# Seven block products for the first projection, and a partial sum that ScalarE copies into PSUM

## The chip, the core and the metric

The kernel runs on one core of a Trainium2 chip. The time is the device time of one execution in microseconds (us); of several runs the median is told. A profile is one execution taken by the hardware profiler. Its engines are PE (TensorE's matrix products), PEld (TensorE's weight loads, which overlap PE), DVE (VectorE), ACT (ScalarE), POOL (GpSimd) and SP, whose queue issues most of the transfers.

## What is computed

Three stages follow each other on 6016 rows of 256 channels; this is the reference without its setup:

```
qn = q / (np.linalg.norm(q, axis=1, keepdims=True) + 1e-06)     # q, k, v: (1, 6016, 256)
kn = k / (np.linalg.norm(k, axis=1, keepdims=True) + 1e-06)
s = kn.transpose(0, 2, 1) @ qn / tau                            # 256 x 256
a = softmax(s)                                                  # over the last axis
x = v @ a                                                       # 6016 x 256
h = x @ w_in                                                    # w_in 256 x 2048
g = np.where(h >= 1, h, np.where(h <= -1, 0, (h + 1) ** 2 / 4))
x = g @ w_out                                                   # w_out 2048 x 256
xn = x / sqrt(mean(x * x, -1) + 1e-6) * rms_g
gate = xn @ w_gate; val = xn @ w_val                            # 256 x 1536 each
out = (gate * sigmoid(gate) * val) @ w_out2                     # w_out2 1536 x 256
```

The weights arrive as doubles and are brought to single precision on the chip. The change concerns `h = x @ w_in` and, to a smaller part, `gate` and `val`.

## The kernel before

**Start.** The scores are summed while q and k arrive; the softmaxed 256 x 256 matrix is multiplied into `w_in`, so that v goes straight through one combined weight, held in SBUF as a rounded part `w1h` and its remainder `w1l`.

**Three products for one.** Every factor is kept as a rounded part and its remainder, and a product of 128 x 128 weights with n columns is three matmuls: high by high, remainder by high, high by remainder. n is the number of rows of one tile: 12 tiles stand in 6 pairs, of which pairs 0 to 4 have n = 512 and pair 5 has n = 448.

**The first network (`network_1`).** For a pair, `prep_v` transposes v on DVE and splits it. `block_A` (line 708) makes one 128 x n block of h from two such products (two blocks of channels, six matmuls), 16 blocks for each tile. Then ACT forms relu(h/2 + 1/2) and squares it, DVE takes max(h, 1) and the smaller of the two (line 722), ACT copies the rounded part `gh`, DVE subtracts for `gl`. `block_B` (line 742) multiplies the block by `w_out` into the sums `y`, two products of three matmuls.

**The second network (`network_2`).** After the norm, `combine` forms from the four blocks of a pair (two channel blocks by two tiles) the seven sums that a seven-product scheme for 2 x 2 blocks needs. For every two blocks of `w_gate` and `w_val` the stored weight has seven blocks too (`to_seven` makes them once and keeps them in DRAM, `load_seven` fetches them). `seven_units` then makes a chain of seven products, p1, p2, p6, p7, p5, p3, p4, in three PSUM buffers: X1 (gx, vx) takes p1, p6, p5 and p3 on top of each other, Z (gz, vz) takes p2, S (gy, vy) takes p7 and p4. In between ACT copies X1 to SBUF (`copied`, line 863) and DVE adds Z or S to a copy (`add`, line 868). A chain gives four blocks: p1 + p2, and three others. `block_D` (line 948) multiplies the gated result by `w_out2`.

**Order.** `ORDER` runs the networks of the pairs in turn: 1 of pairs 0 and 1, 2 of pair 0, 1 of pair 2, 2 of pair 1 and so on. Within a chain the string `CHAIN` sets the wanted order on PE: c is the chain's next product, t one of the two products left over from the chain before (p3, p4), d a product of `block_D`. Every instruction gets a due time; a list planner written into the kernel then places all instructions of PE, ACT, DVE, POOL and SP with its own costs and with buffers from numbered slots (four PSUM slots `mm` for h, X1, Z and S, twenty SBUF slots `tmp`, and others). Each engine executes its instructions in the order so fixed.

Of the kernel before, what the change touches and what calls it, by code (L numbers as in the profile page):

```python
# [15 lines left out]
P = 128  # L16
# [46 lines left out]
def tile_channel_attention_two_ffn(  # L63
# [422 lines left out]
    n_op = {cls: SLOTS[cls] for cls in ("stage", "op", "rows")}  # L486
    first_op = {"stage": 0, "op": n_op["stage"], "rows": n_op["op"] + n_op["stage"]}
# [66 lines left out]
    for t in range(2):  # L554
        V[t] = [Buf("op", f"v{p}{t}", slot=2 * t + i) for i, p in enumerate("hl")]
# [22 lines left out]
    def narrow(key, src, at, step, on_act, into=None):  # L578
        x = Buf("stage", f"wide_{key}", [P, NC, TOK])
# [32 lines left out]
    for p in range(NF2 // 2):  # L612
        kept_dram["wd", p] = drp.tile([P, 4 * C], F32, name=f"kept_wd{p}")
        for nm in "gv":
            kept_dram[nm, p] = drp.tile([P, 2, 7, P], F32, name=f"kept_{nm}{p}")

    def to_rows(kind, j, src, at, step, on_act, eng):
        x = narrow(f"{kind}{j}", src, at, step, on_act)
        w = Buf("rows", f"{kind}{j}", [P, 2, 2, C], F32R)
# [14 lines left out]
    def to_seven(kind, p, src, at, step):  # L634
        f = Buf("stage", f"f{kind}{p}", [P, 8, P])
        h = Buf("stage", f"h{kind}{p}", [P, 7, P], F32R)
        narrow(f"{kind}{p}", src, at, step, True, f)
        for i, (o, a, b, how) in enumerate((
# [9 lines left out]
            at, [(f, s) for s in range(1, 8)], [h], [h])  # L648
# [83 lines left out]
    def block_B(t, f, c, w, at):  # L732
        _, n = tiles[t]
        gh, gl = G[t, f]
        if (f, c) == (0, 0):
            Y[t] = Buf("yo", f"y{t}")
        y = Y[t]

        def mm():
            cs = slice(c * P, (c + 1) * P)  # L740
            for i, (h, x) in enumerate(((0, gh.t), (1, gh.t), (0, gl.t))):
                nc.tensor.matmul(  # L742
                    y.t[:, c, :n], w.t[:, f % 2, h, cs], x[:, :n],
                    start=(f == 0 and i == 0), stop=(f == NF1 - 1 and i == 2),
                )
        op("PE", pe(3, n), mm, at, [gh, gl, (w, 0), (w, 1)], [(y, c)], [y] if (f, c) == (0, 0) else [])
        if (f, c) == (NF1 - 1, NC - 1):
# [7 lines left out]
    def norm(t, at, step):  # L755
# [5 lines left out]
        ps = Buf("mm", f"ms{t}")  # L761
        m = Buf(None, f"m{t}")
# [42 lines left out]
    def combine(q, at, step):  # L805
        _, n = tiles[2 * q]
        x0, x1 = X[2 * q], X[2 * q + 1]
        got = XO[q] = {}
        when = [at]

        def keep(name, b, c=None):
            w = got[name] = Buf("op", f"x{name}_{q}", [P, 2, TOK], F32R)
# [8 lines left out]
        def mix(name, a, b):  # L821
            d = Buf("tmp", f"d{name}_{q}")
# [186 lines left out]
    conversions.sort()  # L1009
# [4 lines left out]
    for due, _, kind, which, src in [c for c in conversions if c[2] in ("wi", "wo")] + late:  # L1014
# [238 lines left out]
```

## Time and profile before

| | |
|---|---|
| median of three runs | 1135.0 us (1134.12 to 1135.71) |
| the profiled execution | 1134.83 us, span of its instructions 1133.1 us |
| PE busy | 1109.2 us, 98% of the span, 4950 instructions |
| PEld, DVE, ACT, POOL busy | 930.7, 820.0, 749.6, 86.4 us |
| granted TensorE clock, mean | 0.994 |

A row of busy time adds up the recorded lengths of instructions. On PE, and to a smaller degree on ACT and DVE, an instruction begins before the recorded end of the one ahead of it, so rates are better read from starts. The matmuls of the scores and of the norms of q and k are recorded as two each, so the profile counts 97 more than the 4853 matmuls of the program.

### The profile page before, as it was taken

The page shows a single profiled execution, that of the slowest core. Times are in us where ns is not written, and L with a number is a line of the kernel's source. Part 1 is how long each engine was busy: PE and PEld are TensorE (multiplying, and loading weights), DVE is VectorE, ACT ScalarE, POOL GpSimd, SP SyncE. Part 2 cuts the span into 40 slices and gives each one's busy share as a digit, 9 for nine tenths or more (in the row PEclk, how much of TensorE's full clock was granted, in tenths as well). Part 3 has the DMA queues.
Part 4 walks back from the last instruction along what each step waited for, and adds up shares of the span by engine and source line. Part 5 has one row for each costly group of instructions (what it writes and reads, how often), then busy time and mean ns, then how long its engine had stood idle before and what let it go on. Part 6 is the DMA issues. An engine that isn't in the chain of part 4 may idle for free.

```text
span 1133.1 us, 13952 instructions
## 1 busy us (share of the span) xinstructions
PE 1109.2 (98%) x4950; PEld 930.7 (82%) x4950; DVE 820.0 (72%) x1311; ACT 749.6 (66%) x1325; POOL 86.4 (8%) x84
## 2 busy tenths in 40 slices
PE   7799999999999999999999999999999999999996
PEld 6678888888888888888888888888888998888995
DVE  5989989969985448886446977445968545976664
ACT  6589898987666666666666556666557566555552
POOL 0000244313100002000000100000200000200000
PEclk9999999999999999999999999999999999999998
DMA  9766575577536413425432432532442412444742
GB/s 346 238 174 180 189 258 217 196 201 260 163 115 185 80 56 135 155 97 123 124 75 102 167 135 53 183 63 89 149 167 103 126 56 92 161 153 155 216 149 33
DMA packets 138854, 167.65 MB, mean 148 GB/s; under 512 B 103712, under 2 KB 103712, under 8 KB 138784
## 3 DMA queue, kind: packets, MB, share of 16 engines
q1 hardware_dynamic: 135072, 166.29, 47.2%
q10 hardware_dynamic: 3712, 0.46, 0.3%
q8 instruction: 39, 0.64, 0.2%
q14 instruction: 31, 0.25, 0.1%
HBM read 142.21 MB, written 24.51 MB: 147 GB/s over the span
## 4 chain that ended last, share of the span: by engine, by line
PE 93%; DMA 4%; DVE 1%; SPq 1%; ACT 0%; issue 0%; DVEq 0%; ACTq 0%
PE y L742 23%; PE h L708 22%; PE o L948 17%; PE vx L855 9%; PE gx L855 9%; PE gy L855 4%; PE vy L855 4%; PE vz L855 2%; PE gz L855 2%; DMA qk<-in_k_dram 1%; DMA wide<-in_moe_w_in_dram 1%; DMA qk<-in_q_dram 1%; PE w_ps L682 1%; SPq L180 1%; DMA soon<-in_moe_w_out_dram 1%; PE w_ps L405 0%
## 5 line engine op out<-in xcount | busy, mean ns | idle before, releaser
L722 DVE SCALAR_TENSOR_TENSOR g<-h,g 128x512 f32<-128x512 f32 (+1 forms) x192 | 129.1, 676 | 144.9 <-ACT g L720 144.9
L742 PE MATMUL y<-gh,wo 128*128 128x512 f32 (+1 forms) x768 | 233.5, 385 | 0.0
L717 ACT ACTIVATE g<-h 128x512 f32<-128x512 f32 (+1 forms) x192 | 112.8, 587 | 121.5 <-PE h L708 121.3
L948 PE MATMUL o<-uh,wd 128*128 128x512 f32 (+1 forms) x576 | 175.6, 386 | 0.0
L742 PEld LDWEIGHTS y<-gh,wo 128*128 128x128 f32 x768 | 144.2, 188 | 27.3 <-DVE wo L143 0.2
L708 PE MATMUL h<-vh,w1h 128*128 128x512 f32 (+1 forms) x384 | 148.1, 386 | 0.3 <-ACT w1h L414 0.3
L708 PE MATMUL h<-vl,w1h 128*128 128x512 f32 (+1 forms) x384 | 148.0, 385 | 0.3 <-DVE vl L143 0.3
L742 PE MATMUL y<-gl,wo 128*128 128x512 f32 (+1 forms) x384 | 148.0, 385 | 0.1
L143 DVE TENSOR_TENSOR gl<-g,gh 128x512 fp32r<-128x512 f32 (+1 forms) x192 | 129.2, 678 | 7.4 <-ACT gh L725 7.1
L948 PEld LDWEIGHTS o<-uh,wd 128*128 128x128 f32 x576 | 108.1, 188 | 20.4
L720 ACT ACTIVATE g<-g 128x512 f32<-128x512 f32 (+1 forms) x192 | 119.0, 621 | 4.2
L725 ACT ACTIVATE gh<-g 128x512 fp32r<-128x512 f32 (+1 forms) x192 | 117.0, 611 | 6.8 <-DVE g L722 6.8
L708 PE MATMUL h<-vh,w1l 128*128 128x512 f32 (+1 forms) x384 | 116.8, 385 | 0.0
L948 PE MATMUL o<-ul,wd 128*128 128x512 f32 (+1 forms) x288 | 111.2, 386 | 1.5 <-DVE ul L143 1.5
L708 PEld LDWEIGHTS h<-vh,w1h 128*128 128x128 f32 x384 | 72.1, 188 | 14.6 <-ACT w1h L414 0.7
L708 PEld LDWEIGHTS h<-vl,w1h 128*128 128x128 f32 x384 | 72.1, 188 | 14.2 <-DVE vl L143 0.6
L742 PEld LDWEIGHTS y<-gl,wo 128*128 128x128 f32 x384 | 72.1, 188 | 13.7 <-DVE gl L143 0.4
L708 PEld LDWEIGHTS h<-vh,w1l 128*128 128x128 f32 x384 | 72.1, 188 | 13.6 <-DVE w1l L415 0.3
L948 PEld LDWEIGHTS o<-ul,wd 128*128 128x128 f32 x288 | 54.1, 188 | 12.1 <-DVE ul L143 1.9
L855 PE MATMUL gy<-xt,gw 128*128 128x512 f32 (+1 forms) x216 | 60.0, 386 | 0.0
L855 PE MATMUL vx<-xt,vw 128*128 128x512 f32 (+1 forms) x216 | 60.0, 386 | 0.0
L855 PE MATMUL gx<-xb,gw 128*128 128x512 f32 (+1 forms) x216 | 60.0, 386 | 0.0
(181 smaller groups left out, 1840.1 us busy)
## 6 DMA issues: line engine op xcount, KB each, us to landing
gw<-kept_g SPq DMA_DIRECT2D x36, 896.0 KB, 4.7
vw<-kept_v SPq DMA_DIRECT2D x36, 896.0 KB, 4.7
wo<-kept_wo SPq DMA_DIRECT2D x40, 512.0 KB, 4.0
wd<-kept_wd SPq DMA_DIRECT2D x36, 512.0 KB, 3.6
vin<-in_v_dram SPq DMA_DIRECT2D x80, 64.0 KB, 3.9
out_dram<-ob SPq DMA_DIRECT2D x80, 64.0 KB, 2.0
qk<-in_q_dram SPq DMA_DIRECT2D x9, 512.0 KB, 10.2
qk<-in_k_dram SPq DMA_DIRECT2D x9, 512.0 KB, 10.2
```

Source lines behind the costliest of these rows:

```text
L143: return eng.tensor_tensor(out=dst_lo, in0=src, in1=hi.bitcast(F32), op=ALU.subtract)
L180: nc.sync.dma_start(out=xv[32 * a:32 * a + 32, c, :n // 32, :], in_=src[a, c])
L682: nc.tensor.matmul(got[b].t, x[:, c * P:(c + 1) * P], w[:, c, :], start=(i == 0), stop=(i == len(terms) - 1),)
L708: nc.tensor.matmul(ps.t[:, :n], w[:, c, f * P:(f + 1) * P], x[:, c, :n], start=(i == 0), stop=(i == len(terms) - 1),)
L717: op("ACT", act(n), lambda: nc.scalar.activation(out=r.t[:, :n], in_=ps.t[:, :n], func=AF.Relu, bias=0.5, scale=0.5), at, [ps], [r], [r])
L720: op("ACT", act(n), lambda: nc.scalar.activation(out=r.t[:, :n], in_=r.t[:, :n], func=AF.Square), at, [], [r])
L722: op("DVE", dve(n), lambda: nc.vector.scalar_tensor_tensor(out=r.t[:, :n], in0=ps.t[:, :n], scalar=1.0, in1=r.t[:, :n], op0=ALU.max, op1=A ...
L725: op("ACT", act(n), lambda: nc.scalar.activation(out=gh.t[:, :n], in_=r.t[:, :n], func=AF.Copy), at, [r], [gh], [gh])
L742: nc.tensor.matmul(y.t[:, c, :n], w.t[:, f % 2, h, cs], x[:, :n], start=(f == 0 and i == 0), stop=(f == NF1 - 1 and i == 2),)
L855: nc.tensor.matmul(ps.t[:, :n], w.t[:, h, a, :], b.t[:, e, :n], start=(start and i == 0), stop=(i == 2), skip_group_check=True,)
L948: nc.tensor.matmul(o.t[:, c, :n], w.t[:, f % 2, h, cs], x[:, :n], start=(nth == 1 and i == 0), stop=(nth == NF2 and i == 2),)
```

## The change

From pair 2 on the first projection uses the scheme of seven products as well. `turn_pair` transposes v of both tiles and `combine` forms the seven sums; `to_seven` makes the seven blocks of each of the eight pairs of weight blocks from `w1h + w1l` (one DVE addition, four on POOL, one copy on ACT, one subtraction on DVE) during the second network of pair 0, writes them to DRAM, and `network_1s` fetches them for each pair and runs eight chains `h` (buffers hx, hz, hy) of seven products. Pairs 0 and 1 keep `network_1`.

In all chains but one (g, pair 4, first) p1 is now copied by ACT into Z's own PSUM buffer, and p2 accumulates onto it, where before p1 was copied to SBUF and DVE added p2. The planner gives such a Z only slots of PSUM that matmuls have already written in at least as many columns (`written`, `seed`). `CHAIN` changes from `ccttccddcdd` to `cttccdcdcdd`, `CHAIN_1` is new, and the slots of the classes `stage` and `op` are merged.

```
-CHAIN = "ccttccddcdd"
-SLOTS = {"mm": 4, "yo": 2, "stage": 7, "op": 19, "rows": 4, "tmp": 20, "seven": 3}
-RESERVE = {"tmp": 4, "mm": 1}
+CHAIN = "cttccdcdcdd"
+CHAIN_1 = "cdttccddcddcddd"
+PLAIN = 2
+H_AT = (70.0, 16.0)
+PREP_S = 50.0
+SLOTS = {"mm": 4, "yo": 2, "op": 24, "rows": 4, "tmp": 20, "seven": 4}
+RESERVE = {"tmp": 4, "mm": 1, "op": 4}
...
-    def to_seven(kind, p, src, at, step):
+    def to_seven(kind, p, at, step, src=None):
...
+            op("DVE", dve(TOK), lambda: nc.vector.tensor_tensor(
+                out=f.t[:, :4, :].rearrange("p (k s) c -> p k (s c)", k=NC),
+                in0=w1h[:, :, cols].bitcast(F32), in1=w1l[:, :, cols].bitcast(F32), op=ALU.add),
...
         def p1(at):
             product(X1, A11, "b11", True, at)
-            copied("a", at)
+            if not seeded:
+                copied("a", at)
+                return
+            Z.seed = n
+            op("ACT", act(n), lambda: nc.scalar.activation(
+                out=Z.t[:, :n], in_=X1.t[:, :n], func=AF.Copy), at, [X1], [Z], urgent=30)

         def p2(at):
-            product(Z, A12, "b21", True, at)
-            take(1, 0, add("a", Z, at), at)
+            product(Z, A12, "b21", not seeded, at)
+            take(1, 0, Z if seeded else add("a", Z, at), at)
...
+    def turn_pair(q, at, step):
...
+            for c in range(NC):
+                op("DVE", dve(n), lambda c=c, x=x, r=r: nc.vector.transpose(
+                    out=r.t[:, c, :n], in_=x.t[:, c, :n]), at, [x], [(r, c)])
+                at += step
+            raw.append(r)
+        combine("v", q, *raw, at, step)
+
+    def network_1s(q):
+        turn_pair(q, phase_at[1, q] - PREP_S, STEP)
...
+                squared(t, f, d, at)
+                for c in range(NC):
+                    pend.append((us, lambda at, c=c: block_B(t, f, c, rows[p], at)))
...
+        for p in range(NF1 // 2):
+            load_seven("h", p, now - LEAD["seven"])
+            rows[p] = load_rows("wo", p, now + LEAD["wd"])
+            chain = seven_units("h", q, p, take(p))
+            fill.extend(pend)
+            pend.clear()
+            for what in CHAIN_1:
...
-        (network_1, network_2)[net - 1](q)
+        if net == 2:
+            network_2(q)
+        elif q < PLAIN:
+            network_1(q)
+            if q == 0:
+                for p in range(NF1 // 2):
+                    to_seven("h", p, phase_at[1, PLAIN] - H_AT[0] + H_AT[1] * p, STEP)
+        else:
+            network_1s(q)
...
-            f = sorted(free[b.cls].values())
+            f = sorted(t for i, t in free[b.cls].items() if b.cls != "mm" or written[i] >= b.seed)
```

Counted in the two built programs, PE has 96 matmuls fewer, ACT 116 instructions more, DVE 37 more, POOL 32 more and SP 48 transfers more. Three places show how the order moves.

PE before, second network of pair 2, from p1 of the gate's fourth chain on (gx_3 and gz_3 are X1 and Z of that chain, vx_2 and vy_2 belong to the chain ahead):

```order
L855 MATMUL gx_3_5917<-xb_2_4613,gw_5810 128x512 x3
L855 MATMUL gz_3_5925<-xb_2_4626,gw_5810 128x512 x3
L855 MATMUL vx_2_5835<-xb_2_4763,vw_5755 128x512 x3
L855 MATMUL vy_2_5869<-xt_2_4753,vw_5755 128x512 x3
L855 MATMUL gx_3_5917<-xt_2_4697,gw_5810 128x512 x3
L855 MATMUL gy_3_5950<-xt_2_4727,gw_5810 128x512 x3
L948 MATMUL o_5649<-uh_2_10_5889,wd_5514 128x512 x2
L948 MATMUL o_5649<-ul_2_10_5921,wd_5514 128x512
L948 MATMUL o_5649<-uh_2_10_5889,wd_5514 128x512 x2
L948 MATMUL o_5649<-ul_2_10_5921,wd_5514 128x512
L855 MATMUL vx_3_5970<-xb_2_4613,vw_5876 128x512 x3
L855 MATMUL gx_3_5917<-xt_2_4704,gw_5810 128x512 x3
```

and the same place after:

```order
L877 MATMUL gx_3_6063<-xb_2_4760,gw_5891 128x512 x3
L975 MATMUL o_5863<-uh_1_11_5987,wd_5613 128x512 x2
L975 MATMUL o_5863<-ul_1_11_6007,wd_5613 128x512
L975 MATMUL o_5863<-uh_1_11_5987,wd_5613 128x512 x2
L975 MATMUL o_5863<-ul_1_11_6007,wd_5613 128x512
L877 MATMUL vx_2_5990<-xb_2_4899,vw_5808 128x512 x3
L975 MATMUL o_5848<-uh_1_00_6024,wd_5613 128x512 x2
L975 MATMUL o_5848<-ul_1_00_6039,wd_5613 128x512
L877 MATMUL vy_2_6048<-xt_2_4891,vw_5808 128x512 x3
L877 MATMUL gz_3_6080<-xb_2_4770,gw_5891 128x512 x3
L877 MATMUL gx_3_6063<-xt_2_4839,gw_5891 128x512 x3
L877 MATMUL gy_3_6116<-xt_2_4870,gw_5891 128x512 x3
```

Before, p1 (to gx_3) and p2 (to gz_3) stood side by side and nine matmuls stood between p1 and p6; now fifteen matmuls stand between p1 and p2, and p6 follows p2.

PE before, first network of pair 3 (h are blocks of the first projection, y the sums of the second):

```order
L708 MATMUL h_3_4951<-vh_4358,w1h 128x512
L708 MATMUL h_3_4951<-vl_4382,w1h 128x512
L708 MATMUL h_3_4951<-vh_4358,w1h 128x512
L708 MATMUL h_3_4951<-vl_4382,w1h 128x512
L708 MATMUL h_3_4951<-vh_4358,w1l 128x512 x2
L742 MATMUL y_4908<-gh_1_4912,wo_4497 128x512 x2
L742 MATMUL y_4908<-gl_1_4931,wo_4497 128x512
L742 MATMUL y_4908<-gh_1_4912,wo_4497 128x512 x2
L742 MATMUL y_4908<-gl_1_4931,wo_4497 128x512
```

and the first network of pair 3 after (hx_4, hz_4 and hy are X1, Z and S of a chain, vb and vt the sums of v):

```order
L877 MATMUL hx_4_5247<-vb_3_4336,hw_5068 128x512 x3
L762 MATMUL y_5062<-gh_4_5225,wo_4931 128x512 x2
L762 MATMUL y_5062<-gl_4_5238,wo_4931 128x512
L762 MATMUL y_5062<-gh_4_5225,wo_4931 128x512 x2
L762 MATMUL y_5062<-gl_4_5238,wo_4931 128x512
L877 MATMUL hx_3_5149<-vb_3_4475,hw_4905 128x512 x3
L762 MATMUL y_5062<-gh_5_5236,wo_4931 128x512 x2
L762 MATMUL y_5062<-gl_5_5251,wo_4931 128x512
L877 MATMUL hy_3_5215<-vt_3_4572,hw_4905 128x512 x3
L877 MATMUL hz_4_5266<-vb_3_4343,hw_5068 128x512 x3
```

Six matmuls to a block of h have given way to single products of a chain, with the products to y in between; fifteen matmuls stand between p1 (to hx_4) and p2 (to hz_4).

ACT before, first network of pair 3 (relu from h, then the square in place, then the rounded part gh):

```order
L725 ACTIVATE gh_8_5200<-g_8_5167 128x512
L717 ACTIVATE g_9_5209<-h_9_5192 128x512
L720 ACTIVATE g_9_5209<-g_9_5209 128x512
L725 ACTIVATE gh_8_5230<-g_8_5188 128x512
L717 ACTIVATE g_9_5239<-h_9_5213 128x512
L720 ACTIVATE g_9_5239<-g_9_5239 128x512
L725 ACTIVATE gh_9_5253<-g_9_5209 128x512
L717 ACTIVATE g_10_5262<-h_10_5243 128x512
L720 ACTIVATE g_10_5262<-g_10_5262 128x512
L725 ACTIVATE gh_9_5274<-g_9_5239 128x512
```

and after, from the second copy of chain 4 to the first copy of chain 5:

```order
L885 ACTIVATE hc_4_5299<-hx_4_5247 128x512
L738 ACTIVATE g_6_5304<-hc_3_5211 128x512
L738 ACTIVATE g_9_5311<-hz_4_5266 128x512
L745 ACTIVATE gh_6_5316<-g_6_5273 128x512
L740 ACTIVATE g_6_5304<-g_6_5304 128x512
L745 ACTIVATE gh_7_5327<-g_7_5287 128x512
L740 ACTIVATE g_9_5311<-g_9_5311 128x512
L885 ACTIVATE hu_4_5336<-hx_4_5247 128x512
L745 ACTIVATE gh_6_5348<-g_6_5304 128x512
L901 ACTIVATE hz_5_5366<-hx_5_5338 128x512
L738 ACTIVATE g_8_5373<-hu_4_5336 128x512
L745 ACTIVATE gh_9_5378<-g_9_5311 128x512
```

A chain has three copies of X1 (to hz, hc and hu) between the three instructions for each of its four blocks; between two copies stand one to six of these.

## Rows read from the trace of the kernel before

**Rows 1.** The page: engines, busy time, share of the span, instructions.

```profile
PE 1109.2 (98%) x4950; PEld 930.7 (82%) x4950; DVE 820.0 (72%) x1311; ACT 749.6 (66%) x1325; POOL 86.4 (8%) x84
```

**Rows 2.** Who waited for whom, PE: us in total, times, longest.

```profile
PE a_ps L457 <- ACT s_sb L451: 6.9, 2, 5.3
PE s_ps L304 <- DMA qk<-in_k_dram: 5.8, 2, 4.3
PE o L948 <- DVE ul L143: 1.5, 1, 1.5
PE h L708 <- ACT w1h L414: 0.3, 1, 0.3
PE h L708 <- DVE vl L143: 0.3, 1, 0.3
PE n_ps L361 <- DVE acc L334: 0.3, 1, 0.3
```

**Rows 3.** Chain that ended last: start us, us; 512, then 448 columns.

```profile
336.03 2.72 PE h L708 x12
341.47 2.72 PE o L948 x12
...
886.84 1.22 PE h L708 x6
888.06 1.22 PE y L742 x6
```

**Rows 4.** Timeline of PE, chains of 448 columns: start us, us, instructions.

```profile
1070.44 0.78 PE L855 MATMUL gy<-xt,gw 128*128 128x448 f32 x3
1071.06 0.78 PE L855 MATMUL vx<-xt,vw 128*128 128x448 f32 x3
```

**Rows 5.** Timeline of PE and ACT around a copy; brackets: idle before, and releaser.

```profile
470.16 0.84 PE L855 MATMUL vx<-xb,vw 128*128 128x512 f32 x3
...
471.10 0.60 ACT L863 ACTIVATE va<-vx 128x512 f32<-128x512 f32 x1 [0.90 <-PE vx L855]
...
472.88 0.84 PE L855 MATMUL vz<-xb,vw 128*128 128x512 f32 x3
```

**Rows 6.** Timeline of ACT where it runs without a gap.

```profile
474.50 0.60 ACT L912 ACTIVATE s<-gx 128x512 f32<-128x512 f32 x1 [1.66 <-PE gx L855]
474.99 0.62 ACT L912 ACTIVATE gu<-gu 128x512 f32<-128x512 f32 x1
475.51 0.59 ACT L863 ACTIVATE vc<-vx 128x512 f32<-128x512 f32 x1
475.99 0.63 ACT L924 ACTIVATE uh<-va 128x512 fp32r<-128x512 f32 x1
476.52 0.63 ACT L912 ACTIVATE gc<-gc 128x512 f32<-128x512 f32 x1
```

**Rows 7.** Busy time by stretch: first network of pairs 0, 2, 5.

```profile
core 0: us, PE busy (x) PEld busy (x) DVE busy (x) ACT busy (x) POOL busy (x), PEclk, DMA share, GB/s
73.00:168.00 95.00, 95.00 (x421) 78.67 (x420) 90.90 (x155) 86.75 (x158) 19.32 (x22) 1.00 0.66 209
345.00:433.00 88.00, 88.00 (x390) 72.88 (x389) 43.81 (x69) 56.22 (x97) 0.00 (x0) 1.00 0.40 103
877.00:955.00 78.00, 78.00 (x382) 71.40 (x381) 39.11 (x67) 48.66 (x93) 0.00 (x0) 1.00 0.29 80
```

**Rows 8.** Groups by form: busy us, mean ns | idle before.

```profile
L863 ACT ACTIVATE ga<-gx 128x512 f32<-128x512 f32 x30 | 17.9, 595 | 26.6 <-PE gx L855 26.6
L912 ACT ACTIVATE ga<-ga 128x512 f32<-128x512 f32 x30 | 18.9, 629 | 6.2 <-DVE ga L868 6.1
```

**Rows 9.** Transfers: issues, KB each, median us to landing.

```profile
gw<-kept_g SPq DMA_DIRECT2D x36, 896.0 KB, 4.7
```

**Rows 10.** Busy time by stretch, as Rows 7: a slow start, the end.

```profile
56.00:60.00 4.00, 2.65 (x8) 2.17 (x9) 3.66 (x11) 1.25 (x4) 0.00 (x0) 0.50 0.01 4
1120.00:1124.00 4.00, 3.13 (x15) 2.87 (x16) 2.65 (x6) 0.58 (x1) 0.00 (x0) 1.00 0.00 0
```

**Rows 11.** Timeline of PE in the slow stretch.

```profile
57.69 2.06 PE L405 MATMUL w_ps<-wi,ah 128*128 128x512 f32 x4
59.55 1.05 PE L405 MATMUL w_ps<-wi,al 128*128 128x512 f32 x2
```

More of the change, by code (lines that the diff above doesn't have):

```diff
@@ L821, in mix @@
         def mix(name, a, b):
-            d = Buf("tmp", f"d{name}_{q}")
+            d = Buf("tmp", f"d{kind}{name}_{q}")
             ap = lambda y: y[0].t[:, y[1], :n] if isinstance(y, tuple) else y.t[:, :n]
@@ L1013, in tile_channel_attention_two_ffn @@
         late[i] = (phase_at[2, 0] * first + (c[0] - phase_at[2, 0] * first) * (i + 1) / len(late),) + c[1:]
-    for due, _, kind, which, src in [c for c in conversions if c[2] in ("wi", "wo")] + late:
+    rest = [c for c in conversions if c[2] not in ("g", "v", "wd")]
+    for due, _, kind, which, src in sorted(rest + late, key=lambda c: c[:2]):
         at = max(0.0, due - SLACK)
@@ L1022, in tile_channel_attention_two_ffn @@
         else:
-            to_seven(kind, which, src, at, STEP)
+            to_seven(kind, which, at, STEP, src)
     def network_1(q):
@@ L1058, in network_1, with take, made @@
             push(*m1.pop(0))
-        for t in ts:
-            last_t[t] = now
-    last_t = {}
+    def turn_pair(q, at, step):
+        _, n = tiles[2 * q]
+        raw = []
+        for t in (2 * q, 2 * q + 1):
+            x = Buf("op", f"vin{t}", [P, NC, TOK])
+            r = Buf("op", f"vr{t}", [P, NC, TOK])
+            op("SP", dma(512, 8), lambda x=x, t=t: dma_v(x.t, t), at - LEAD["v"], writes=[x])
+            for c in range(NC):
[6 more added lines that the diff above has]
+        turn_pair(q, phase_at[1, q] - PREP_S, STEP)
+        n = tiles[2 * q][1]
+        us = pe(3, n)[0]
+        def take(p):
+            def made(i, k, d, at):
+                t, f = 2 * q + k, 2 * p + i
+                squared(t, f, d, at)
+                for c in range(NC):
+                    pend.append((us, lambda at, c=c: block_B(t, f, c, rows[p], at)))
+            return made
+        rows = {}
+        for p in range(NF1 // 2):
[5 more added lines that the diff above has]
+            for what in CHAIN_1:
+                if what == "d":
+                    pop_fill(1)
+                elif what == "t":
+                    if tail:
+                        unit(us, tail.pop(0))
+                else:
+                    unit(us, chain.pop(0))
+            tail.extend(chain)
+        while tail:
+            unit(us, tail.pop(0))
+            pop_fill(1)
+        fill.extend(pend)
+        pend.clear()
     def network_2(q):
@@ L1066, in network_2 @@
         at = end_at[1, q] + NORM_AT
-        while fill and (1, q) == before:
-            pop_fill(1)
         for i in range(2):
             norm(2 * q + i, at + i * NORM_GAP, STEP)
-        combine(q, max(at + NORM_GAP + 15 * STEP, phase_at[before] + 8), STEP)
+        combine("x", q, X[2 * q], X[2 * q + 1], max(at + NORM_GAP + 15 * STEP, phase_at[before] + 8), STEP)
         us = pe(3, tiles[2 * q][1])[0]
@@ L1181, in tile_channel_attention_two_ffn @@
                     best = key, o
+        if best is None:
+            print({cls: [(b.name, b.users) for b in {id(b): b for o in ops for b, _, _ in o.uses}.values() if b.cls == cls and b.t is not None and b.users] for cls in SLOTS})
+            print({cls: [b.name for b in q[:3]] for cls, q in queue.items()})
         assert best is not None, [(e, [(o.seq, o.at, [b.name for b in o.new]) for o in p[:4]]) for e, p in pending.items()]
@@ L1192, in tile_channel_attention_two_ffn @@
             f = free[b.cls]
-            b.slot = min((i for i in f if f[i] <= t), key=lambda i: (f[i], i))
+            mm = b.cls == "mm"
+            b.slot = min(
+                (i for i in f if f[i] <= t and not (mm and written[i] < b.seed)),
+                key=lambda i: (mm and written[i], f[i], i),
+            )
             del f[b.slot]
```

74 lines of the change are left out of this document (46 added, 28 removed).

## The prediction

> **What bounds the kernel now.** I read the page first: PE is busy for 1109.2 of 1133.1 us, ACT for 749.6, DVE for 820.0 [rows 1]. A busy share says little while recorded matmuls overlap, so the second view is who waited for whom. PE's whole list has six entries and 15.1 us [rows 2]; five of them name tiles of the start (scores, norms, the first blocks of h), and one is left for all the rest, 1.5 us for `ul` near the end. So from the start's end at about 72 us to 1120 us nothing ends later than TensorE's own stream: every matmul that goes away there is time, unless a wait comes in its place. The third view, the chain that ended last, gives the price. Twelve matmuls of 512 columns take 2.72 us, 0.2267 us each, in `block_A` as in `block_D`; six of 448 columns take 1.22 us, 0.203 each, in the first network of pair 5 [rows 3]. In the chains of pair 5 three of 448 columns take 0.62 us from start to start, 0.207 each [rows 4].
>
> **The change, part by part.**
>
> *Matmuls that go.* A pair's first projection is 32 blocks of six matmuls, 192; with chains it is 8 times 7 products of three, 168. That is 24 less for each of pairs 2 to 5, 96 in all, as the built programs have it. Pairs 2 to 4: 72 x 0.2267 = 16.3 us. Pair 5: 24 x 0.203 = 4.9 us if the pitch stays; if its chains run at the 0.207 of [rows 4], 192 x 0.203 - 168 x 0.207 = 4.2 us; if its 192 matmuls to y take that pitch too, 0.8 less, 3.4 us. I take 4.2, since the new matmuls are chains. Together 20.5 us, between 19.7 and 21.2, and all of it on the path.
>
> *The second product's new wait.* In 103 chains (71 of g and v, 32 of h) p2 must now wait for ACT's copy of p1. The trace has a place that stands just as the new order wants it: p1 (vx) starts at 470.16, the copy runs from 471.10 and takes 0.60, so it is done at 471.70, and nine matmuls after p1 the next vz product starts at 472.88 [rows 5]. From p1's start to the end of the copy are 1.54 us; with three matmuls of p1 and nine others the cover is 12 x 0.2267 = 2.72 us, so 1.1 us are left. In the new order 45 of the 103 chains have nine matmuls between p1 and p2, 57 have more, one has three (the second v chain of pair 0): there 6 x 0.2267 = 1.36 us of cover against 1.54, a wait of about 0.2 us. The kernel before already has ties of this kind: p6 overwrites X1 only after the copy, with nine matmuls of cover in 39 of its 72 chains and six in five, and PE waited for none of them [rows 2]. I therefore cost the tie at 0.2 us. Queued behind a waiting p2 is all of PE, so cover that fails is paid in full.
>
> *The copy's length.* No row has ACT writing to PSUM. The nearest rows are 0.595 us from PSUM to SBUF and 0.629 from SBUF to SBUF [rows 8]; I take 0.60. Bounds of 0.5 and 0.8 leave the cover of 1.1 us standing, so it costs nothing either way.
>
> *Work added to ACT.* 116 instructions: 96 copies in the h chains, 8 of the new weight blocks, 12 in `combine`. Back to back ACT starts one every 0.505 us (474.50 to 476.52 in four steps) although each is recorded at about 0.61 [rows 6]. An h chain has 7 x 3 + 8 x 3 = 45 matmuls, 10.2 us on PE, and 12 + 3 = 15 instructions on ACT, 7.6 us, 1.47 to the microsecond. In the first network of pair 0 ACT had 158 in 95 us, 1.66 to the microsecond, and PE was busy for all 95 [rows 7]. So the new load is under one that the trace has shown without a wait. What hides it is PE's own stream; if that cover failed it would be by single late copies, the first rival. The densest spot of the new order is in pair 2, where 21 of ACT's instructions stand beside one chain of 10.2 us: 21 x 0.505 = 10.6 us, 0.4 late, within the cover of 1.1. I put 0.3 us for such places.
>
> *DVE and POOL.* DVE loses 71 additions of p2 and gains 64 in the h chains, 16 for the new weights and 28 in turning and summing v: 37 more, 93 in a first network of some 82 us. Pair 0 had 155 in 95 us with PE full [rows 7]. POOL's 32 additions serve the weights only. Nothing here is on the path.
>
> *Transfers.* 48 more on SP: 16 writes of the new blocks and 32 loads of 896 KB, each due 16 us ahead of its chain. Like loads land 4.7 us after their issue [rows 9]. Eight loads are 7.3 MB in about 80 us, 92 GB/s on top of the 103 of [rows 7]; pair 0 moved 209 GB/s with PE full. They cost nothing if SP isn't held up; what stands behind a held load on SP is the next weights, 16 us ahead of use.
>
> *Ends.* PE's order in the last 50 rows is the old one with other line numbers, so the 1.5 us wait and what follows stay. The start differs in the order of a few conversions, and PE's order is the same through the start.
>
> **Sum.** 1134.83 (the profiled execution) - 20.5 + 0.2 + 0.3 = 1114.8 us. The median of the runs lies 0.17 above the profiled execution: 1115.0 us.
>
> **Rivals.**
>
> *ScalarE slips a little in the h chains.* ACT is in order, and relu, square and rounding of four blocks stand between the copies, some of them waiting for DVE. For it: 15 instructions at their recorded 0.61 us would be 9.2 of 10.2 us, and the copies hold PSUM slots longer than before, four slots for X1, Z and S of a chain and X1 of the next. Against it: [rows 6] and [rows 7]. If each of the 32 h chains waits 0.2 to 0.3 us, 6 to 10 us are lost: 1121 to 1125 us.
>
> *Slower: the copy to Z behind three other instructions.* From p1's start the copy ends after 1.54 us; with two more instructions ahead of it after 2.55, still under 2.72; with three after 3.06, and p2 waits 0.34 us. In all 103 chains that is 35 us, 1150 us. The point from which it decides is 20.5 / 103 = 0.2 us a chain. For it: in the new ACT order up to six instructions stand between a copy and the one before it. Against it: ACT was waiting 0.90 us for PE before the copy of [rows 5], and the same copies held p6 up nowhere.
>
> *The new weights come late.* They are made in the second network of pair 0 and must be in DRAM and back before pair 2. If SP or DVE is behind, the first chains wait for a landing each, 4.7 us [rows 9], once or twice: 1120 to 1125 us.
>
> *The clock.* At the start PE waits for several microseconds and the granted clock of 56 to 60 us is 0.50, that is 1.2 GHz; matmuls of 512 columns then start every (59.55 - 57.69) / 4 = 0.465 us, 0.24 more than at 2.4 GHz [rows 10, 11]. 86 of them would eat the whole gain: about 1135 us, no change. After the wait of 1.5 us near the end the granted clock is 1.00 [rows 2, 10], so single short waits don't bring it. The Trainium skill, TensorE: Matmul & The Clock Gate, section A second HAM failure mode: psum-queue depth-cycling, says that a kernel that goes round its PSUM buffers can idle so often between groups of matmuls that the clock swings between its two levels, which speaks against a tie inside a chain. By that rule the clock of an h stretch would fall; the trace does not agree so far, as it goes round the same four buffers at 1.00 in [rows 7].
>
> **How the numbers follow.** The forecast (1113 to 1117) has 0.72; ScalarE slipping 0.11; late weights 0.06; slower by late copies 0.05, and 0.01 for other ways to slower; the clock at about no change 0.03; 0.02 for a little more than forecast, if pair 5 gives 4.9 us and the end shortens. The range of 1112.5 to 1122 holds the forecast, the little more, half of the late weights and a third of the slipping, about 0.8. Runs of this kernel tell a difference of about 0.2% from none, 2.3 us. Faster: 0.72 + 0.11 + 0.06 + 0.02 = 0.91. The same: 0.03. Slower: 0.06.
>
> **What would show it.** In the profile after, PE should count 4854, 96 less, and its list of waits should have nothing new over 1 us after 72 us. The stretches of the first networks from pair 2 on should be about 5.4 us shorter with PE full and the clock at 1.00, and ACT should be busier there. If p2 waits for `hz`, `gz` or `vz` from ACT in the list, the tie was mis-costed; if waits for `hw` from DMA stand there, the loads; if ACT's copies into PSUM take over 1 us, their length. The prediction is wrong if PE is full and the time still is not 20 us less: then the pitch of a matmul has risen.

## The result, and the profile after

| | before | after |
|---|---|---|
| median, same chip (4 runs each) | 1134.6 us (1134.12 to 1135.71) | 1116.85 us (1116.51 to 1118.6) |
| the profiled execution; its span | 1134.83; 1133.1 us | 1116.51; 1114.7 us |
| granted clock, mean | 0.994 | 0.994 |

The ratio is 0.9845, 95% interval 0.9828 to 0.9862: faster by 17.8 us. Forecast were 1115.0 us and a range of 1112.5 to 1122.0. On another chip the changed kernel gave 0.9835 (0.982 to 0.9849).

The page's engines after, to be read beside [rows 1]:

```profile
PE 1090.5 (98%) x4854; PEld 912.8 (82%) x4854; DVE 847.4 (76%) x1348; ACT 797.6 (72%) x1441; POOL 103.6 (9%) x116
```

PE counts 4854 matmuls, 96 fewer, as the two programs say. Who waited for whom, PE, from 72 us to the end (total us, times, longest), beside [rows 2], where the wait for `ul` is the one that is not of the start:

```profile
PE o L975 <- DVE ul L147: 1.5, 1, 1.5
PE vx L877 <- DVE vc L890: 0.5, 1, 0.5
PE o L975 <- DVE ob L986: 0.4, 2, 0.2
PE vz L877 <- ACT vz L901: 0.2, 1, 0.2
```

The old wait for `ul` is still there; three entries are new, and none is over 1 us. Busy time by stretch, columns as in [rows 7]: first networks of pairs 2, 3 and 5 after.

```profile
345.00:425.00 80.00, 79.99 (x353) 65.90 (x353) 54.88 (x86) 64.92 (x120) 5.07 (x8) 1.00 0.66 200
515.00:595.00 80.00, 80.00 (x355) 66.24 (x354) 50.96 (x81) 63.14 (x119) 0.00 (x0) 1.00 0.63 170
850.00:925.00 75.00, 75.00 (x366) 68.45 (x365) 49.90 (x88) 58.95 (x120) 0.00 (x0) 1.00 0.55 170
```

PE still does 4.4 matmuls to the microsecond at a clock of 1.00 (353 in 80 us, 390 in 88 before). ACT has 120 instructions in 80 us, 1.50 to the microsecond, and PE waits for none of them there. The new weights are not all made in the second network of pair 0: the DVE additions that begin them start from 237 to 354 us, two of the eight after the first h chain has begun at 332 us (POOL's x8 in the first row is their eight additions).

**Where the time went.** Recorded lengths of matmuls (0.39 us) overlap, so the list of waits shows little of a wait shorter than 0.16 us. I therefore went through the starts of all matmuls from the first product to y to the last matmul of the program. What a step takes up to 0.2268 us (512 columns) or 0.2075 (448) counts as matmul, and the rest as wait:

| us, one profiled execution each | before | after |
|---|---|---|
| first y to last matmul | 1053.1 | 1035.1 |
| of it matmuls | 1049.4 | 1028.3 |
| of it waits | 3.7 | 6.9 |

Matmuls give 21.1 us, waits take 3.2 back. The new waits stand at seven places (start is that of the matmul ahead of the wait; lost adds up the wait and the late start of the second matmul behind it):

| start, us | waiting | for | lost, us |
|---|---|---|---|
| 262.7 | vz, a p2 | ACT's copy to vz | 0.46 |
| 350.7 | hy | DVE's sum hu, which frees a PSUM slot | 0.28 |
| 513.2, 685.9 | o | DVE's ob, likewise | 0.40 each |
| 956.5 | vx, a p1 | DVE's sum vc, likewise | 0.82 |
| 1026.6, 1029.7 | o | DVE's ob, likewise | 0.47 each |

Only the first is the tie that the change makes. Timeline of PE, then of ACT there (start us, us, instruction; in brackets idle before and what ended it):

```profile
261.50 0.86 PE L877 MATMUL vx<-xb,vw 128*128 128x512 f32 x3
262.20 0.85 PE L877 MATMUL gx<-xt,gw 128*128 128x512 f32 x3
263.23 0.98 PE L877 MATMUL vz<-xb,vw 128*128 128x512 f32 x3 [0.18 <-ACT vz L901]
...
261.57 0.94 ACT L661 ACTIVATE hh<-fh 128x896 fp32r<-128x896 f32 x1
262.60 0.58 ACT L901 ACTIVATE vz<-vx 128x512 f32<-128x512 f32 x1
```

This is the chain with three matmuls of cover. p1 ends at 262.36, but ACT is on `hh`, the rounded part of a new weight block, until 262.5; the copy ends at 263.18 and p2 starts 0.05 later. The largest new wait is for DVE, in the second network of pair 4; PE, then DVE:

```profile
956.00 0.84 PE L877 MATMUL gy<-xt,gw 128*128 128x512 f32 x3
957.39 0.96 PE L877 MATMUL vx<-xb,vw 128*128 128x512 f32 x3 [0.55 <-DVE vc L890]
...
955.52 0.69 DVE L947 TENSOR_TENSOR s<-s,vx 128x512 f32<-128x512 f32 x1 [0.37 <-PE vx L877]
956.13 0.64 DVE L817 STREAM_TRANSPOSE sb<-sa 128x448 f32<-128x448 f32 x1
956.69 0.65 DVE L890 TENSOR_TENSOR vc<-vy,vc 128x512 f32<-128x512 f32 x1
957.26 0.66 DVE L820 SCALAR_TENSOR_TENSOR x<-x,rg,sb 128x448 f32<-128x448 f32 x1
```

p1 of the new chain needs a PSUM slot, vy holds it until DVE has added it to vc, and that addition stands behind a gate's product (`s`) and a transposition of pair 5's norm (`sb`). It ends at 957.34 and PE goes on at 957.39.

### The profile page after: what moved, and what is told of

It is laid out like the page before. It is cut to its first block, busy times and chain, and to the rows that moved or that the text cites. A ratio compares the mean times of both kernels' runs of the same rounds, so it can differ in the third digit from the quotient of the medians.

```text
span 1114.7 us, 13997 instructions
## 1 busy us (share of the span) xinstructions
PE 1090.5 (98%) x4854; PEld 912.8 (82%) x4854; DVE 847.4 (76%) x1348; ACT 797.6 (72%) x1441; POOL 103.6 (9%) x116
## 4 chain that ended last, share of the span: by engine, by line
PE 92%; DMA 4%; DVE 3%; SPq 1%; ACT 0%; issue 0%; DVEq 0%; ACTq 0%
PE y L762 23%; PE o L975 17%; PE gx L877 8%; PE vx L877 8%; PE hx L877 7%; PE h L724 7%; PE vy L877 4%; PE gy L877 4%; PE hy L877 4%; PE vz L877 2%; PE gz L877 2%; PE hz L877 2%; DMA qk<-in_k_dram 1%; DMA wide<-in_moe_w_in_dram 1%; DMA qk<-in_q_dram 1%; PE w_ps L697 1%
## 5 line engine op out<-in xcount | busy, mean ns | idle before, releaser
L147 DVE TENSOR_TENSOR gl<-g,gh 128x512 fp32r<-128x512 f32 (+1 forms) x192 | 133.6, 701 | 30.0 <-ACT gh L745 29.9
L877 PE MATMUL vx<-xb,vw 128*128 128x512 f32 (+1 forms) x216 | 60.1, 386 | 0.5 <-DVE vc L890 0.5
L877 PE MATMUL gx<-xt,gw 128*128 128x512 f32 (+1 forms) x216 | 59.9, 386 | 0.0
L877 PE MATMUL vy<-xt,vw 128*128 128x512 f32 (+1 forms) x216 | 59.9, 386 | 0.0
L809 POOL TENSOR_SCALAR m<-sb 128x16 f32<-128x16 f32 (+1 forms) x12 | 5.0, 416 | 585.3 <-DVE sb L807 585.0
L890 DVE TENSOR_TENSOR hc<-hy,hc 128x512 f32<-128x512 f32 (+1 forms) x32 | 21.5, 673 | 45.1 <-PE hy L877 45.1
L890 DVE TENSOR_TENSOR vu<-vy,vu 128x512 f32<-128x512 f32 (+1 forms) x36 | 24.3, 676 | 37.7 <-ACT vu L885 37.4
L877 PE MATMUL hy<-vt,hw 128*128 128x512 f32 (+1 forms) x192 | 52.9, 384 | 0.0
L877 PE MATMUL hx<-vt,hw 128*128 128x512 f32 (+1 forms) x192 | 52.8, 383 | 0.0
```

Source lines behind the costliest of these rows:

```text
L147: return eng.tensor_tensor(out=dst_lo, in0=src, in1=hi.bitcast(F32), op=ALU.subtract)
L809: nxt("POOL", pool(0.3), lambda: nc.gpsimd.tensor_scalar(out=m.t[:, :nb], in0=s1.t[:, :n].rearrange("p (b j) -> p b j", j=32)[:, :, 0], sc ...
L877: nc.tensor.matmul(ps.t[:, :n], w.t[:, h, a, :], b.t[:, e, :n], start=(start and i == 0), stop=(i == 2), skip_group_check=True,)
L890: op("DVE", dve(n), lambda: nc.vector.tensor_tensor(out=d.t[:, :n], in0=b.t[:, :n], in1=d.t[:, :n], op=ALU.add), at, [b], [d], urgent=20)
```

## The experiments

The ratios are to the kernel before on the same chip. The medians come from four sets of runs, in which the kernel before took 1133.4 to 1134.6 us, so between rows they compare to about 1 us only. "Matmuls" and "waits" are the two parts of the stretch from first y to last matmul, as above, in each run's profiled execution (pair1 has 24 matmuls fewer, and in ease_pe six more stand ahead of the first y).

| kernel | median, us | ratio (95%) | matmuls | waits |
|---|---|---|---|---|
| before | 1134.6 | | 1049.4 | 3.7 |
| after | 1116.85 | 0.9845 (0.9828 to 0.9862) | 1028.3 | 6.9 |
| seeds_only | 1135.47 | 1.0019 (1.0009 to 1.0029) | 1048.1 | 5.7 |
| seven_only | 1121.87 | 0.9898 (0.9881 to 0.9914) | 1028.1 | 12.6 |
| two_pairs | 1126.91 | 0.9941 (0.9926 to 0.9956) | 1037.9 | 6.9 |
| pair1 | 1159.83 | 1.0234 (1.0218 to 1.0249) | 1021.6 | 55.2 |
| copy_x2 | 1117.8 | 0.9859 (0.9844 to 0.9874) | 1028.2 | 8.0 |
| copy_x3 | 1129.91 | 0.9973 (0.9962 to 0.9984) | 1027.1 | 20.2 |
| copy_x4 | 1176.66 | 1.0381 (1.0364 to 1.0399) | 1027.5 | 66.8 |
| ease_pe | 1121.58 | 0.9892 (0.9876 to 0.9908) | 1025.6 | 11.7 |
| seed_h | 1121.26 | 0.9881 (0.9864 to 0.9898) | 1026.8 | 13.6 |
| seed_h_old | 1121.12 | 0.9881 (0.9866 to 0.9896) | 1026.9 | 13.1 |
| seed_gv | 1118.3 | 0.9855 (0.9839 to 0.9872) | 1028.3 | 8.1 |
| changed_again | 1115.77 | 0.9835 (0.982 to 0.9849) | 1028.3 | 6.9 |

**The two halves of the change, each alone.** Without seven products in the first projection, but with the copies into Z, the new CHAIN and the merged slots:

```
-PLAIN = 2
+PLAIN = 6
-            if q == 0:
+            if q == 0 and PLAIN < NPAIR:
```

> All six pairs keep the first projection in blocks of six matmuls; the seeds (ScalarE copies p1 into Z, p2 accumulates) and the new chain string stay in the chains of the second network, and the order is planned anew. My theory: the seeds take nothing off TensorE and their wait is covered, so 1134.6 us within 1.5, with 4950 matmuls in the profile. Rival: the seeds carry part of the gain, since DVE loses 71 additions: 1125 to 1131 us. Second rival: their tie costs, 1137 us or more, with waits for vz and gz in PE's list.

And the other half, with p2 added by DVE as before:

```
-        seeded = (kind, q, p) != ("g", NPAIR - 2, 0)
+        seeded = False
```

> The seven products from pair 2 on stay; no chain is seeded, p1 is copied to SBUF and DVE adds p2 in all 104 chains; planned anew. My theory: the matmuls carry the whole gain, 1117 us within 2, with 4854 matmuls; DVE has 103 additions more than with seeds, so the small waits for DVE may grow by 1 or 2 us. Rival: without the seeds DVE can't keep up beside the h chains, where it then has 24 additions a pair more: 1122 us or more, with waits for DVE in PE's list.

Measured: the copies alone lose 1.8 us against the kernel before (waits 2.0 us more), though DVE falls to 783.6 us busy. By the starts, three waits for ACT's copy to vz or gz make 0.95 us of that, and four other waits for ACT (three for `x`, one for `gu`) 1.1 us; the new string and the merged slots are in this kernel too, and no run parts them from the copies. The seven products alone gain 11.8 us: my 1117 us missed, and the rival's 1122 with waits for DVE came. So the seven products carry the gain, and the copies are worth 5 to 6 us more, but only beside them. The trace of seven_only says where. PE's waits after 72 us, then busy time by stretch around the passage from the second network of pair 0 to the first of pair 2:

```profile
PE o L975 <- DVE ul L147: 2.5, 2, 1.6
PE o L975 <- DVE ob L986: 2.4, 1, 2.4
PE y L762 <- ACT x L769: 1.7, 2, 0.9
PE hy L877 <- DVE s L947: 0.6, 1, 0.6
```

```profile
320.00:334.00 14.00, 14.00 (x63) 11.56 (x62) 14.00 (x21) 10.47 (x20) 7.55 (x9) 1.00 0.75 250
334.00:346.00 12.00, 7.51 (x32) 5.23 (x30) 12.00 (x20) 7.55 (x13) 3.07 (x3) 1.00 0.74 268
346.00:350.00 4.00, 4.00 (x12) 3.21 (x13) 3.86 (x6) 2.37 (x4) 0.87 (x2) 0.66 0.65 96
```

DVE is busy for all 26 us up to 346 and PE waits for it three times. Behind the third wait the clock falls: 0.66 over 346 to 350 us, where seven starts of matmuls lie 0.43 us apart and nine matmuls lose 1.6 us together. POOL has a part in DVE's lateness. While it adds up a new weight (330.24 to 333.69 us), the same subtraction on DVE takes longer:

```profile
321.70 0.69 DVE L147 TENSOR_TENSOR ul<-va,uh 128x512 fp32r<-128x512 f32 x1
...
330.69 0.95 DVE L147 TENSOR_TENSOR ul<-va,uh 128x512 fp32r<-128x512 f32 x1
```

Added up over what the same lines take where POOL is idle, DVE's recorded lengths are 1.4 us longer from 320 to 346 us here and 0.4 in the changed kernel: an estimate of POOL's part. The same stretches in the changed kernel, with the copies:

```profile
320.00:334.00 14.00, 14.00 (x64) 11.59 (x63) 13.86 (x21) 9.89 (x19) 2.54 (x4) 1.00 0.91 309
334.00:346.00 12.00, 12.00 (x55) 9.94 (x54) 11.01 (x19) 10.11 (x18) 0.00 (x0) 1.00 0.63 200
346.00:350.00 4.00, 4.00 (x19) 3.34 (x18) 4.00 (x8) 2.87 (x5) 1.46 (x2) 1.00 0.80 118
```

**Half the dose.** Seven products from pair 4 on.

```
-PLAIN = 2
+PLAIN = 4
```

> The seven products only for pairs 4 and 5, blocks of six for pairs 0 to 3. My theory, a price per matmul: 24 x 0.2267 + 24 x 0.203 = 10.3 us off 1134.6 and about 1.5 us of small waits back: 1125.8 us. Rival: the loss against the sum comes from the h chains themselves, then half the loss, 1125.8 as well, but with waits inside the two h stretches; if it comes from making the new weights early on, the loss of the changed kernel is in the second network of pair 0, and here it moves to before pair 4.

48 matmuls go, 24 of each length, 10.3 us at their pitch. The gain is 6.8 us (8.8 were expected), and the waits are 3.1 us more than in the kernel before. The waits are as large as with four pairs (6.9) and stand at places of the same kind (vz for ACT in pair 0, vx for vc in pair 4, o for ob in pair 5). So they are no toll on each h chain: most stand in the second networks, and the two further pairs with seven products, which the changed kernel has, bring 5.5 us each, about their whole price. That the new order there makes the waits is likely, but no run shows it by itself.

**One pair more.** Seven products from pair 1 on, with the weights made earlier to be in time.

```
-PLAIN = 2
-H_AT = (70.0, 16.0)
-PREP_S = 50.0
+PLAIN = 1
+H_AT = (22.0, 10.0)
+PREP_S = 36.0
```

> The seven products from pair 1 on, the new weights made during the first network of pair 0 (due 22 us ahead of pair 1, one more every 10 us). My theory: 24 matmuls less, 5.4 us, on top of the changed kernel: 1111.4 us if the weights are in time. Rival: ScalarE and DVE are fullest just there (158 and 155 instructions in 95 us), the weights come late, PE waits for hw or for ScalarE in pair 1, and the time is 1117 us or more.

24 matmuls fewer, and 43 us slower than the changed kernel. PE's waits between 140 and 300 us (the three largest), and busy time by stretch:

```profile
PE y L762 <- DVE gl L147: 12.4, 9, 3.3
PE hz L877 <- ACT hz L901: 6.2, 3, 2.8
PE hx L877 <- ACT hc L885: 3.6, 1, 3.6
```

```profile
145.00:160.00 15.00, 13.28 (x53) 10.34 (x52) 15.00 (x23) 11.39 (x20) 6.69 (x8) 0.91 0.60 208
160.00:175.00 15.00, 8.60 (x20) 4.96 (x19) 13.93 (x20) 7.38 (x12) 8.87 (x11) 0.61 0.59 209
175.00:190.00 15.00, 7.87 (x16) 4.32 (x16) 13.67 (x15) 8.41 (x13) 14.08 (x16) 0.50 0.83 279
```

The weights' additions and subtractions are put where the first network of pair 0 fills DVE ([rows 7]: 90.9 of 95 us). DVE falls behind, PE waits, and the clock goes to its lower level, 1.2 GHz at 0.50; between 157 and 229 us it falls four times and comes back each time. The two largest waits for ACT (2.8 and 3.6 us) lead to the same work: ACT waits for POOL's additions, 1.75 us here and 4.11 before 183 us, and the copy of X1 stands behind the weights' copies:

```profile
176.67 0.95 ACT L661 ACTIVATE hh<-fh 128x896 fp32r<-128x896 f32 x1 [1.75 <-POOL fh L657]
177.53 0.95 ACT L661 ACTIVATE hg<-fg 128x896 fp32r<-128x896 f32 x1
178.38 0.58 ACT L901 ACTIVATE hz<-hx 128x512 f32<-128x512 f32 x1
```

The loads are the small part: PE's list has one wait of 1.1 us for `hw`.

**The tie, made longer.** The copy to Z issued two, three and four times (the same values each time); here twice:

```
-            op("ACT", act(n), lambda: nc.scalar.activation(
-                out=Z.t[:, :n], in_=X1.t[:, :n], func=AF.Copy), at, [X1], [Z], urgent=30)
+            op("ACT", act(n), lambda: [nc.scalar.activation(
+                out=Z.t[:, :n], in_=X1.t[:, :n], func=AF.Copy) for _ in range(2)], at, [X1], [Z], urgent=30)
```

> The changed kernel in its own order, but every copy of p1 into Z is made twice in a row; the plan does not know of it. The copy in the trace ends 1.5 us after p1 starts, with a second one 0.5 us later at 2.0, under the cover of 2.72 us that 45 chains of 512 or 448 columns have and the others exceed. My theory: 0.5 to 2 us over the changed kernel, 1117.5 to 1119 us. Rival: the tie already ends last in most chains, then 0.5 us in 103 chains, 50 us: 1165 us.

> The same with three copies. The last ends about 2.5 us after p1 starts: just under 2.72 us for chains of 512 columns with nine matmuls of cover, just over 2.48 for those of 448. My theory: 3 to 8 us over the changed kernel, 1120 to 1125 us, mostly in pair 5. Rival of a tie without cover: 100 us.

> The same with four copies. The last ends 3.0 us after p1 starts, past the cover: 45 chains wait some 0.35 us and lose 0.1 more at the restart, 20 us; ScalarE is also later for the other copies. My theory: 1132 to 1142 us, a step well above that from two to three copies. Rival: no step, the same amount for each copy.

Against the changed kernel's 1116.85: 1.0, 13 and 60 us more (by the ratios 1.6, 14.5 and 61). Twice came as the theory had it; three and four times cost far more than the theory's 3 to 8 and 15 to 25, though the step from three to four was foretold. From the trace after, the time between the end of the copy and the start of p2 in all 103 chains: 0.05 us in the v chain above, then 0.58 and 0.78, 33 chains under 1.25, median 1.34. A repeated copy is recorded at 0.61 us more (1.20, 1.81 and 2.42 for two, three and four), not at the 0.505 of [rows 6] that the expectations used; and the cover of 2.72 us that the first of them gives to all 45 chains is 2.48 for those of 448 columns, as the second has it. Each chain's slack less 0.61, 1.23 and 1.84 us, with 0.05 from the copy's end to the start and 0.11 for the first matmul after a wait (below), adds up to 0.9, 11.9 and 49 us. The waits grew by 1.1, 13.3 and 60; of the 60, some 56 are for the copies, so about 7 us of them are more than this count gives and were not taken apart. In copy_x4, PE's waits after 72 us and one of them, PE and ACT:

```profile
PE vz L877 <- ACT vz L901: 19.4, 33, 2.1
PE gz L877 <- ACT gz L901: 7.5, 16, 0.6
PE hz L877 <- ACT hz L901: 4.9, 11, 1.0
```

```profile
485.76 0.39 PE L975 MATMUL o<-ul,wd 128*128 128x512 f32 x1
486.63 0.96 PE L877 MATMUL vz<-xb,vw 128*128 128x512 f32 x3 [0.48 <-ACT vz L901]
...
484.15 2.42 ACT L901 ACTIVATE vz<-vx 128x512 f32<-128x512 f32 x4 [0.86 <-PE vx L877]
```

So the rival of the copy behind three others is a real mechanism: past some 1.2 us of delay the slack of most chains is gone at once, and PE pays. In the changed kernel its condition is not there. The clock does not join in: with all these waits it is granted at 1.00 from 72 to 1160 us of copy_x4.

**PE's due times.** If the small waits come from a planner that takes PE for too fast, PE's allowance for lateness, raised in the planner, should dissolve them.

```
-EASE = {"PE": 0.2, "ACT": 0.8, "DVE": 0.8, "POOL": 0.2, "SP": 0.2}
-HURRY = {"PE": 0.2, "ACT": 0.1, "DVE": 0.1, "POOL": 0.0, "SP": 0.0}
+EASE = {"PE": 0.7, "ACT": 0.8, "DVE": 0.8, "POOL": 0.2, "SP": 0.2}
+HURRY = {"PE": 0.7, "ACT": 0.1, "DVE": 0.1, "POOL": 0.0, "SP": 0.0}
```

> The changed kernel planned with 0.7 us instead of 0.2 between a result of ScalarE or DVE and the matmul that needs it, nothing else changed: PE takes another ready product first where it can. My theory: the seven small new waits of PE (3.3 us with their restarts) are places where DVE and ScalarE are later than planned, so most of them go: 1114 to 1116 us. Rival: they are set by PSUM buffers coming free, and the time stays at 1116.8 within 0.7 or grows.

It is 4.7 us slower than the changed kernel. Waits move and multiply: 41 starts of matmuls are over 0.03 us late, where 16 were; one of 1.1 us comes as early as 176 us. The theory fell and the rival's number held; its reason, PSUM slots, covers a part only, since the largest waits listed are for results of DVE (ul, sb, sl). Another order has other collisions, and this one number does not take the seven away.

**Which copies pay?** Three kernels beside the changed one. Copies in the h chains alone:

```
-        seeded = (kind, q, p) != ("g", NPAIR - 2, 0)
+        seeded = kind == "h"
```

> The changed kernel, but only the 32 h chains have p2 on top of ScalarE's copy; the 71 chains of gate and value add p2 on DVE again, as before. Theory: without any copies into PSUM the kernel was at 1121.9 us, and all it lost lay beside the h chains, where DVE has most to do; so the h chains alone bring the whole of that back, and the second network's ties cost as much (some 1.8 us when they were made alone) as they save. Forecast 1115.5 to 1118 us, a ratio of 0.983 to 0.9855 to the kernel before. Rival: the copies pay in the second network, where DVE is freed of 71 additions; then this kernel stands near 1121 us, 0.988.

The same with the old string:

```
-CHAIN = "cttccdcdcdd"
+CHAIN = "ccttccddcdd"
-        seeded = (kind, q, p) != ("g", NPAIR - 2, 0)
+        seeded = kind == "h"
```

> As the run before, and CHAIN is the old string again (p1 and p2 of a gate or value chain side by side), which is free to be so since no p2 of gate or value waits for a copy any more. CHAIN_1 of the h chains stays. Theory: the copies and the new string cost about 1.8 us in the second network, as they did when they were made alone; both are gone here: 1114 to 1117 us, 0.982 to 0.9845 of the kernel before. Rival: DVE's 71 additions are back and its late releases of PSUM slots after the h chains grow: 1118 to 1121 us, 0.985 to 0.988.

And copies in the gate and value chains alone:

```
-        seeded = (kind, q, p) != ("g", NPAIR - 2, 0)
+        seeded = kind != "h" and (kind, q, p) != ("g", NPAIR - 2, 0)
```

> The mirror: gate and value chains have p2 on top of ScalarE's copy as in the changed kernel, the 32 h chains add p2 on DVE. Theory: the loss of the kernel without copies lay beside the h chains and stays: 1121 to 1124 us, 0.988 to 0.991. Rival: what DVE saves in the second network is what counts: near 1117 us, 0.984 to 0.986.

Beside them the changed kernel once more, with no edit:

> The changed kernel once more, with nothing altered, so that the three kernels beside it have their reference on the same chip. 1116 to 1118 us, a ratio of 0.983 to 0.9862; all theories agree.

My theory fell. With copies in the h chains alone the kernel stands at 1121.3 us, as with none; with copies in gate and value alone at 1118.3, near its rival; and the old string changes nothing. Busy time of seed_h in the passage, then of seed_gv:

```profile
334.00:346.00 12.00, 8.64 (x36) 6.17 (x34) 12.00 (x19) 7.87 (x14) 3.22 (x3) 1.00 0.85 292
346.00:350.00 4.00, 2.87 (x7) 2.32 (x8) 3.45 (x6) 1.46 (x2) 2.04 (x4) 0.53 0.41 62
```

```profile
334.00:346.00 12.00, 12.00 (x54) 9.93 (x54) 11.01 (x19) 10.48 (x20) 0.00 (x0) 1.00 0.58 192
346.00:350.00 4.00, 4.00 (x19) 3.30 (x19) 4.00 (x7) 2.90 (x7) 0.00 (x0) 1.00 0.80 118
```

What pays is the copies in the second network of pair 0. There most of the new weights are made and the first v is turned; DVE has no room, as the stretch of 265 to 305 us shows, before and after:

```profile
265.00:305.00 40.00, 40.00 (x178) 33.07 (x177) 39.16 (x65) 27.03 (x48) 10.88 (x11) 1.00 0.53 175
```

```profile
265.00:305.00 40.00, 40.00 (x178) 33.07 (x177) 39.87 (x64) 28.55 (x50) 13.38 (x15) 1.00 0.59 198
```

The kernel before had DVE free again by 335 us (6.83 of the next 10 us); the new work fills that. Copies into PSUM take the twelve additions of pair 0's chains from DVE, 0.60 us each from start to start, 7.2 us. Without that DVE is late: PE loses 6.9 us in seven_only between 334 and 351 us, of it 5.0 in three waits for DVE, 0.3 in the matmuls behind them and 1.6 by the lower clock. Outside that passage seven_only waits 5.6 us in all, less than the changed kernel's 6.6. No run has the copies in pair 0 alone; that they pay there is read from the place of the loss. In the kernel without new weights the same copies free DVE for nothing, and that kernel loses 1.8 us. Whether the copies in the h chains pay is not settled: 2.5 us lie between the medians of seed_gv and changed_again, 1.4 between their profiled executions, and the intervals overlap.

None of the variants beats the changed kernel.

## Why the prediction held, step by step

*What bounds it.* Right. PE is full at 1.00 after the start in both kernels but for the few us of waits, and the matmuls that went are the gain.

*Matmuls that go.* The terms were right for pairs 2 to 4. Pair 5's was taken too small: its chains run at 0.2027 us a matmul in the first network, not at the 0.207 of [rows 4], so it gives 4.9 us and not 4.2. The pitch belongs to the stretch, not to the chain. The sum is 21.2 us, the upper bound.

*The tie.* Right: nine matmuls of cover were to leave 1.1 us, and the trace has 1.07 to 1.34 there, but for one chain with 0.58; the one chain with three was to wait 0.2 us, and it lost 0.46, since a copy for the new weights was in the way and the restart costs too.

*The copy's length.* 0.60 taken, 0.584 measured. Copies of X1 after, to PSUM and to SBUF (busy us, mean ns | idle before):

```profile
L901 ACT ACTIVATE vz<-vx 128x512 f32<-128x512 f32 x30 | 17.5, 584 | 12.6 <-PE vx L877 11.6
```

```profile
L885 ACT ACTIVATE vc<-vx 128x512 f32<-128x512 f32 x30 | 17.9, 596 | 15.4 <-PE vx L877 15.4
```

The Trainium skill, ScalarE: Activation LUTs, section Step-by-step: what each stage is for, says that ScalarE writes faster to PSUM than to SBUF. The trace agrees, by 12 ns, which moves nothing here.

*ACT.* No h chain waits for a copy; the least slack there is 0.78 us. The 0.3 us for dense places was too much for ACT.

*DVE at nothing.* This is the step that was wrong, in its size and in its argument. I compared the first networks only ([rows 7]), where DVE has room. Most of the new weights are made in a second network, where DVE was at 39.16 of 40 us already, and POOL's additions, which I put at nothing too, make DVE slower beside them. Six of the seven new waits are for DVE, 2.8 us. Only one of them (350.7 us) is near the new weights; the others stand from 513 us on, and what made DVE late there stays open. That no more was lost where the weights are made is the work of the copies, which I had costed as a tie alone and not as 7.2 us of relief: seven_only, without them, stands at 1121.87, at the end of my range. The two omissions, DVE's new work and DVE's relief, went opposite ways, and that they nearly cancelled there is luck: the range held by it. For all new waits together I had 0.5 us, and 3.2 came.

*The sum again.* 1114.8 us forecast for the profiled execution, 2.7 more for waits, 0.6 less for matmuls (21.1 instead of 20.5), 0.4 less since the first y came earlier: 1116.5, and 1116.51 was measured. That the matmuls are the gain was right; the term that was mis-sized is the one for waits.

*Transfers.* Right. All 32 loads land as the old ones did, and PE waits for none:

```profile
hw<-kept_h SPq DMA_DIRECT2D x32, 896.0 KB, 4.6
```

*Rivals.* ScalarE slipping in the h chains: didn't come. Copies behind three others: not here, but real (copy_x4). Late weights: their transport was not late (but for 1.1 us in pair1), their making was the danger (pair1, seven_only). The clock: 1.00 in the changed kernel, and the seven waits, all under 1 us, did not move it; it fell where PE waited 1.6 and 2.4 us close together (seven_only) and in pair1, where it was busy for 13.3 of 15 us and then for 8.6 of 15. The rule of the Trainium skill that the prediction named (TensorE: Matmul & The Clock Gate, A second HAM failure mode: psum-queue depth-cycling) has no case in the changed kernel, which goes round its PSUM slots at 1.00, nor in copy_x4, where 80 waits for a copy into a PSUM slot, of up to 2.3 us, left the clock at 1.00. In seven_only the third wait was for a PSUM slot and the clock did fall behind it, once, and came back.

## What to carry to other kernels

Where an engine is full, price a removed instruction on it at its pitch from start to start; here that gave 20.5 us, and 17.8 came. Ask of the other engines not whether they have room on average but whether they have it in the stretch where the new work is put, the preparation of new weights above all: a load moved off such an engine there can be worth more than the dependency that it costs. A tie between engines is free as long as its slack lasts; count the slack of every instance, since most of them have the same, and they fail together.

## What the runs showed of the hardware

- After a wait of PE the second matmul starts 0.11 us late too, whatever the wait's length (0.104 to 0.114 behind the eight waits of the changed kernel, of 0.17 to 1.66 us, at a clock of 1.00): a wait of 0.17 us costs 0.28.
- Matmuls of 448 columns run at one of two pitches, 0.2027 or 0.2067 us on average, for long stretches. In the changed kernel the longer one holds from the wait that ends at 1030 us to the one that ends at 1102.6 us, 339 of 759 matmuls, in both executions; in ease_pe no stretch has it, and in copy_x3, whose PE order is that of the changed kernel, none either. That is worth 1.4 us; what chooses it stays open. Most of what the table's matmuls differ by, beyond their counts, is this.
- The same copy of ScalarE repeated into the same buffer takes 0.61 us more each time; instructions on different buffers start each 0.505 us ([rows 6]).
- A DVE subtraction of 128x512 in SBUF (line 147) is recorded at 0.71 us at most where POOL is idle (309 of them in seven_only after 72 us), and at up to 0.95 beside POOL's additions (line 657), as at 330.69 us.
